# A retention and SoLU kernel: w_in cast without a stride, rows of w_out grouped anew, a new order of the instructions

## The chip, the cores and the metric

The kernel runs on one core of a Trainium2 chip. The time is in device microseconds, from the first instruction to the last, as the median of several runs. PE is TensorE (matmuls; its weight loads are shown as PEld), DVE is VectorE, ACT is ScalarE, POOL is GpSimd, and SP is the engine whose queue issues nearly all DMAs here. Each engine works through its own queue in the order in which it was given its instructions and waits for the others by semaphores.

## What is computed

```python
scores = (1 / np.sqrt(64)) * np.matmul(q, k.transpose(0, 1, 3, 2))   # 8 x 8 heads, 576 x 64
gamma = 1.0 - 2.0 ** (-5.0 - np.arange(8))
Dmat = np.where(rel >= 0, gamma[:, None, None] ** rel, 0.0)           # rel = i - j
attn = np.matmul(scores * Dmat, v)
x = attn.transpose(0, 2, 1, 3).reshape(4608, 512)

h = x @ w_in                                    # 512 -> 1024
e = np.exp(h - h.max(-1, keepdims=True))
solu = h * (e / (e.sum(-1, keepdims=True) + 1e-09))
mu, var = mean and variance of solu along the row
out = ((solu - mu) / np.sqrt(var + 1e-06) * g_ln) @ w_out           # 1024 -> 512
```

All inputs and the output are float32. The order of the 1,024 hidden columns doesn't matter to the result as long as w_in's columns, g_ln and w_out's rows follow the same one.

## The kernel before

The 576 positions of a batch are cut into two blocks of 256 and a tail of 64. A *pair* is one block of one batch (two times 128 rows of the output), or the tails of four batches together; there are 18 pairs, n = 0 to 17, and in each i = 0, 1 stands for its 128 rows. Attention is done in chunks with a carried state: for a block the scores inside a chunk, masked with the powers of gamma, and the contribution of the state.

All work is cut into named steps, and one string, `ORDER` (line 744), gives the order of all of them: `k:0.1@g` is step `k` for pair 0, half 1, on engine g (v is VectorE, s ScalarE, g GpSimd). The program runs through the string and issues each step's instructions, so each engine's queue is the string's words for that engine. `BANKS` (line 840) gives the PSUM banks in the same order. The steps that matter here:

- loads, on SP's queue: `lq`, `lk`, `lv` (line 173, 512 KB of rows of 512 bytes each, into 16 buffers `ld` used in turn), `wi` (line 647, a 512 KB slice of w_in, rows of 4 KB), `wo` (line 667, a quarter of w_out), `st` (results), `dt` and `du` (transposes by DMA)
- `q`, `k`, `v` (line 197 with a table of powers of gamma, line 152 or 150 without): casts from float32 to float16
- `tp` and `qkT`: transposes of q and k on PE and their copies out of PSUM; `sc`: scores on PE (line 265); `mk`: the masks on VectorE (line 276); `kp`, `t`, `s32`, `s16`: the state; `xs`, `xv`: x from state and from scores on PE; `xT`: its copy
- `cwA`, `cwB`: casts of the two halves of a slice of w_in
- `mm1` (line 426): h, eight matmuls of 512 columns per 128 rows, over four slices of w_in; `max` (line 434) and `solu` (line 497) on VectorE, `exp` (line 449) and `sq` (line 517) on ScalarE, `nmu`, `w1`, `w2`, `pow`: small ones for the row's mean and variance
- `lpj` and `uTj`: transposes of the result and their copies; `mm2` (line 607): the second product; `osb`: its scaling out of PSUM
- `ws`, `mean`, `mc`, `cw`: w_out times g_ln, its mean over the rows, and the difference, so that the row's mean needn't be taken off later. For the first three pairs, where `cw` isn't done yet, `uc` takes the mean off the row.
- `warm:k`: k matmuls of 512 columns on zeros; `gx`: a table by Exp on ScalarE; `small`: the tables of powers; `gln`: g_ln, with `g32` its multiple

Hidden column 8f + c is kept at place 128c + f: so w_in's cast reads with a stride of 8 numbers, and partition p of w_out holds the rows 8p + c, two of which are 4 KB without a gap. The casts, the load of w_out and the first loads read so:

```python
653:         copy(eng, w_in16[:, a, 512 * i : 512 * i + 512].rearrange("p (c f) -> p c f", c=4), src)
666:         w = moe_w_out.rearrange("(p c) m -> p c m", p=P)
850:         nc.scalar.dma_start(out=small, in_=nc.inline_tensor(small_np, name="small_c").ap())
851:         nc.scalar.dma_start(out=gln, in_=moe_g_ln.rearrange("(p c) -> p c", p=P))
```

Of the kernel before, what the change touches and what calls it, by code (L numbers as in the profile page):

```python
# [46 lines left out]
def kernel(  # L47
# [684 lines left out]
    def gx_(n, i, j, eng):  # L732
# [23 lines left out]
        xs:2.1 max:1.0 xT:2.1@s solu:1.1 mm1:2.0 lpj:0 q:3.1@g max:2.0 wo:2 wo:0 v:3.0@g g32
        k:3.1@g exp:1.0 mm1:2.1 solu:1.0 ws:4@s k:3.0@s wo:1 exp:2.0 w1:0@g v:3.1@g ws:0@g wo:3
        ws:1@g ws:5@g ws:2@s w2:0 uTj:0.1@v uTj:0.0@v ws:3@s max:2.1 lk:4 w1:1@v nmu:1.1 nmu:1.0
        ws:6@s warm:4 kp:3 ws:7@g t:3.0@s tp:3 solu:2.0 uc:1.0@v mm2:0.0 s32:3.0 qkT:3.0@s exp:2.1
        s32:2.1 qkT:3.1@s lv:4 pow:0 t:3.1 k:4.1@s sq:1.0 mean k:4.0@g sc:3.1 sc:3.0 solu:2.1  # L760
        nmu:2.0 mm2:0.1 v:4.1@v mc@s mk:3.1.0 mk:3.1.1 s16:3.0@g v:4.0@g lk:5 lk:6 mk:3.0.1
        mk:3.0.0 sq:1.1 uc:1.1@s tp:4 s32:3.1 kp:4 lq:5 qkT:4.0@s cw:5@g xv:3 qkT:4.1@s osb:0.1@v
        xs:3.1 t:4.0 warm:4 lpj:1 xT:3.1@s lq:6 cw:6@v sc:4.0 k:6.1@g nmu:2.1 xT:3.0@v s32:4.0
        k:5.1@g lv:5 uTj:1.1@s s16:1.1@s cw:0@v uTj:1.0@s osb:0.0@s t:4.1 mk:4.0.0 uc:2.0@v mm1:3.0
        w2:1 k:5.0@g q:5.1@g mm1:3.1 q:5.0@g pow:1 v:5.0@g s16:4.0@g max:3.0 uc:2.1@v s32:4.1 lk:7
        sc:4.1 q:6.0@s q:6.1@s mk:4.0.1 v:5.1@g mm2:1.0 exp:3.0 max:3.1 st:0.1 lv:6 mk:4.1.0
        mk:4.1.1 mm2:1.1 xv:4 w1:2@g xs:4.1 v:6.0@g solu:3.0 k:6.0@s v:6.1@g osb:1.0@s exp:3.1
        solu:3.1 dt:5 kp:5 t:5.0 osb:1.1@s xs:4.0 tp:6 st:1.0 s16:2.1@g cw:1@v st:0.0 sq:2.0 kp:6
        xT:4.1@s t:6.0 warm:2 lpj:2 s32:5.0 qkT:6.1@v t:5.1 xT:4.0@s qkT:6.0@s uTj:2.1@s cw:4@g
        sc:5.1 sc:5.0 uTj:2.0@s nmu:3.1 lq:8 mk:5.1.1 cw:7@v mk:5.1.0 sq:3.1 k:7.0@s sq:2.1 cw:3@v  # L770
        mk:5.0.0 mm1:4.0 max:4.0 lv:8 cw:2@g w2:2 pow:2 s32:6.0 mm1:4.1 s16:5.0@g exp:4.0 s16:6.0@g
        lq:7 mm2:2.1 lv:7 max:4.1 mk:5.0.1 solu:4.0 t:6.1 mm2:2.0 exp:4.1 k:7.1@s xs:5.1 xs:5.0
        osb:2.1@s solu:4.1 q:7.1@g sc:6.0 q:7.0@g osb:2.0@s mk:6.0.1 xv:5 v:7.1@v lk:8 lq:9 sc:6.1
        lpj:3 xT:5.0@s mm1:5.0 mk:6.1.0 uTj:3.0@s mk:6.0.0 mk:6.1.1 xs:6.0 lpj:4 nmu:3.0 w1:3@v
        max:5.0 uTj:3.1@s sq:3.0 xT:5.1@s xv:6 dt:7 xT:6.0 w2:3 xs:6.1 s32:5.1 q:8.0@g q:8.1@g
        mm2:3.1 v:8.0@g st:1.1 v:7.0@g nmu:4.1 mm2:3.0 w1:4@g k:8.1@g pow:3 q:9.0@g exp:5.0 xT:6.1
        uTj:4.1@v kp:7 uTj:4.0@s k:8.0@s lk:10 solu:5.0 osb:3.0@s nmu:5.0 sc:7.0 s16:5.1@g tp:8
        t:7.0 osb:3.1@s mm1:5.1 mk:7.0.0 sq:5.0 qkT:8.0@v nmu:4.0 sq:4.1 qkT:8.1@s sq:4.0 sc:7.1
        mk:7.0.1 lv:9 s32:7.0 mm1:6.0 max:5.1 exp:5.1 s16:7.0@g mk:7.1.1 mk:7.1.0 max:6.0 lk:9
        st:2.0 exp:6.0 st:2.1 s16:4.1@g q:9.1@g s16:3.1@g mm2:4.0 xs:7.0 s32:6.1 t:7.1 w2:4 pow:4  # L780
        mm2:4.1 st:3.0 lq:11 k:9.0@s osb:4.0@s solu:5.1 solu:6.0 xv:7 nmu:5.1 sc:8.1 osb:4.1@s
        nmu:6.0 mk:8.1.0 sq:5.1 sc:8.0 lq:10 xs:7.1 xT:7.0@s w1:5@g v:9.0@g lv:10 mm1:6.1 v:9.1@g
        k:10.1@g mk:8.0.1 s16:6.1@g s32:7.1 w2:5 mk:8.0.0 lpj:5 mm1:7.0 xT:7.1@s q:10.1@g max:6.1
        uTj:5.1@s exp:6.1 uTj:5.0@v sq:6.0 k:9.1@g k:10.0@g max:7.0 exp:7.0 mm2:5.1 mm2:5.0
        s16:7.1@g pow:5 v:8.1@g osb:5.1@s solu:6.1 lpj:6 kp:9 st:3.1 lk:11 dt:9 osb:5.0@s nmu:6.1
        mk:8.1.1 xv:8 solu:7.0 xs:8.1 t:9.0@v uTj:6.1@v sq:6.1 xT:8.1@s xs:8.0 st:4.1 lv:11 nmu:7.0
        v:10.0@g k:11.1@g q:10.0@g s32:9.0 tp:10 t:9.1 sc:9.1 mm1:7.1 xT:8.0@s v:10.1@g q:11.1@g
        qkT:10.0@s qkT:10.1@v uTj:6.0@s mk:9.1.0 mk:9.1.1 w1:6@g sc:9.0 kp:10 mm1:8.0 max:7.1
        mk:9.0.0 w2:6 t:10.0@s mk:9.0.1 lq:13 lk:12 s16:9.0@s q:11.0@g k:11.0@g s32:10.0 v:11.1@g
        max:8.0 s32:9.1 xs:9.1 v:11.0@g exp:7.1 t:10.1 mm2:6.1 pow:6 st:5.0 s16:10.0@g w1:7@g  # L790
        solu:7.1 sq:7.0 exp:8.0 mm2:6.0 k:12.1@s st:4.0 sc:10.1 solu:8.0 osb:6.1@v xv:9 mk:10.1.1
        mk:10.1.0 osb:6.0@s k:12.0@g xT:9.1@s nmu:7.1 lq:15 xT:9.0@s lpj:7 mm1:8.1 uTj:7.0@s kp:11
        uTj:7.1@v dt:11 sq:7.1 t:11.0@s st:5.1 lq:12 max:8.1 sc:10.0 mm1:9.0 w2:7 mk:10.0.1 exp:8.1
        mk:10.0.0 solu:8.1 pow:7 mm2:7.1 max:9.0 xv:10 xs:10.1 mm2:7.0 xT:10.0 s32:10.1 q:12.1@g
        xT:10.1 s32:11.0 q:13.0@g q:12.0@g q:13.1@g sc:11.1 w1:8@v osb:7.1@s lpj:8 exp:9.0 solu:9.0
        t:11.1 tp:12 lv:13 s16:11.0@s osb:7.0@s mk:11.1.1 uTj:8.0@s nmu:8.1 mm1:9.1 nmu:8.0 sc:11.0
        mk:11.1.0 uTj:8.1@s lv:12 qkT:12.0@v qkT:12.1@v v:12.0@g v:12.1@g kp:12 sq:8.1 max:9.1
        t:12.0@s st:6.1 st:7.1 mk:11.0.1 mk:11.0.0 v:13.1@g mm1:10.0 sq:8.0 max:10.0 s32:11.1
        exp:9.1 mm2:8.0 lk:14 st:6.0 mm2:8.1 s32:12.0 w2:8 t:12.1 xs:11.1 pow:8 solu:9.1 s16:9.1@s
        exp:10.0 sc:12.0 w1:9@g lk:13 lq:14 lk:15 lq:16 osb:8.0@s osb:8.1@s nmu:9.0 solu:10.0  # L800
        mk:12.0.0 xv:11 k:13.0@g xT:11.0@v sc:12.1 mk:12.1.0 xT:11.1@s mk:12.0.1 q:14.1@g k:14.1@g
        mk:12.1.1 lpj:9 k:13.1@g s16:11.1@s mm1:10.1 k:15.0@g v:13.0@g uTj:9.0@s uTj:9.1@s mm1:11.0
# [110 lines left out]
```

## Time and profile before

| | |
|---|---|
| median of 3 runs | 213.36 us (212.89 to 214.8) |
| profiled execution | 214.05 us, its span 212.3 us |
| PE busy | 196.4 us (93%) |
| DVE busy | 186.1 us (88%) |
| ACT busy | 171.0 us (81%) |
| POOL busy | 143.6 us (68%) |
| DMA | 49.29 MB in 90,530 packets, 232 GB/s in the mean |
| granted PE clock, mean | 0.983 |

The profile is of one execution. Busy time is the time in which an engine had an instruction in work; a busy PE is not a PE at its peak. The chain of waits is followed back from the last instruction: at each step to what released it, or to the instruction ahead of it on its engine. A group is a set of like instructions with the busy time, the mean of one in ns and the idle time just before them with its releaser. In a stretch, (x45) counts the instructions that began in it, and the three last columns are the clock that PE was granted, the busy share of the DMA engines and GB/s.

### The profile page before, as it was taken

Reading aid. Unit: us, or ns where it says so; the run is one execution under the profiler, and the core shown is the slowest. Engines: PE = TensorE matmul, PEld = TensorE weight load, DVE = VectorE, ACT = ScalarE, POOL = GpSimd, SP = SyncE. Lnnn points to the kernel's source line nnn. Section 1 sums busy time; section 2 is a strip of 40 time slices with the busy share of each in tenths; the row PEclk is TensorE's granted clock in tenths of the full one; section 3 lists DMA queues with packets and bytes.
Section 4 is the critical chain, followed back from the end, with each engine's and each line's share of the span. In section 5 each row is a group of like instructions: output and inputs, shape, how many; then the busy total and the mean of one; then the engine's idle time right before and its main releaser. Section 6 shows DMA issues by size and latency. Waiting matters only on the chain.

```text
span 212.3 us, 7613 instructions
## 1 busy us (share of the span) xinstructions
PE 196.4 (93%) x3154; PEld 103.2 (49%) x3154; DVE 186.1 (88%) x335; ACT 171.0 (81%) x288; POOL 143.6 (68%) x223
## 2 busy tenths in 40 slices
...
GB/s 162 290 383 310 281 296 367 295 259 262 138 217 183 213 209 216 320 293 223 249 327 164 285 236 316 279 197 246 264 203 217 238 99 179 171 148 115 85 198 150
DMA packets 90530, 49.29 MB, mean 232 GB/s; under 512 B 29440, under 2 KB 84992, under 8 KB 90496
## 3 DMA queue, kind: packets, MB, share of 16 engines
...
q10 hardware_dynamic: 368, 0.11, 0.4%
...
## 4 chain that ended last, share of the span: by engine, by line
PE 70%; DVE 14%; DMA 4%; SPq 4%; issue 3%; ACT 2%; POOL 1%; ACTq 0%; DVEq 0%; POOLq 0%
PE psum L426 25%; PE psum L607 24%; PE psum L265 5%; DVE nm L434 4%; PE psum L364 4%; DMA ld<-in_moe_w_in_dram 4%; PE psum L349 3%; PE psum L584 3%; SPq L173 3%; DVE u L497 2%; PE psum L290 2%; PE psum L239 1%; SPq L647 1%; PE psum L726 1%; DVE uc L553 1%
## 5 line engine op out<-in xcount | busy, mean ns | idle before, releaser
L426 PE MATMUL psum<-w_in,xT 128*128 128x512 f16 x280 | 68.5, 390 | 1.6 <-issue 0.7
L607 PE MATMUL psum<-w_out,uTj 128*128 128x512 f16 (+1 forms) x248 | 55.1, 372 | 0.0
L434 DVE TENSOR_REDUCE nm<-psum 128x1 f32<-128x1024 f32 x35 | 42.5, 1218 | 6.5 <-PE psum L426 6.1
L449 ACT ACTIVATE e<-psum,nm 128x1024 f32<-128x1024 f32 x35 | 39.0, 1114 | 11.0 <-DVE nm L434 9.2
L607 PEld LDWEIGHTS <-uTj 128*128 128x128 f16 x296 | 28.0, 98 | 31.0 <-issue 0.6
L497 DVE SCALAR_TENSOR_TENSOR u<-psum,e 128x1024 f16<-128x1024 f32 x35 | 42.0, 1216 | 0.4 <-ACT e L449 0.3
L517 ACT ACTIVATE sq<-u,nmu 128x1024 f16<-128x1024 f16 x35 | 40.3, 1150 | 1.2 <-DVE nmu L507 0.9
L426 PEld LDWEIGHTS <-xT 128*128 128x128 f16 x280 | 25.8, 100 | 31.3 <-issue 4.7
L540 POOL TENSOR_TENSOR rs<-w,mhalf 128x2 f32<-128x2 f32 x17 | 11.8, 696 | 38.0 <-DVE w L528 36.7
L197 POOL TENSOR_TENSOR v<-ld,small 128x512 f16<-128x512 f32 x29 | 30.4, 1057 | 4.6 <-DMA ld<-in_v_dram 3.5
L197 POOL TENSOR_TENSOR qk<-ld,small 128x512 f16<-128x512 f32 x24 | 25.0, 1050 | 1.1 <-DMA ld<-in_q_dram 0.6
L150 ACT COPY uTj<-psum 128x1024 f16<-128x1024 f16 (+1 forms) x18 | 17.3, 990 | 3.1 <-PE psum L584 3.1
L314 POOL TENSOR_TENSOR s32a<-t,small 128x256 f32<-128x256 f32 x16 | 10.6, 662 | 11.8 <-DVE t L152 6.9
L726 PE MATMUL psum<-s16s 128*128 128x512 f16 x50 | 14.2, 429 | 3.5 <-DVE s16s L853 3.1
L152 POOL CAST qk<-ld 128x512 f16<-128x512 f32 x25 | 15.4, 628 | 0.7 <-DMA ld<-in_k_dram 0.6
L150 ACT COPY qkT<-psum 128x1024 f16<-128x1024 f16 x12 | 12.0, 1018 | 4.7 <-PE psum L239 4.7
L265 PE MATMUL psum<-qkT 64*64 64x128 f16 x576 | 14.7, 223 | 0.2
L150 ACT CAST xT<-psum 128x512 f16<-128x512 f32 x24 | 13.3, 588 | 1.7 <-PE psum L349 1.0
L265 PEld LDWEIGHTS <-qkT 64*64 64x64 f16 x576 | 9.8, 107 | 7.5 <-issue 6.3
L364 PEld LDWEIGHTS <-v 64*64 64x64 f16 x576 | 9.3, 106 | 7.1 <-issue 6.8
L349 PE MATMUL psum<-qkT,s16s 128*128 128x128 f16 (+1 forms) x128 | 10.7, 216 | 1.6 <-POOL s16s L152 1.4
L314 POOL TENSOR_TENSOR s32b<-t,small 128x256 f32<-128x256 f32 x16 | 10.2, 640 | 2.0 <-DVE t L305 1.8
...
## 6 DMA issues: line engine op xcount, KB each, us to landing
...
```

The lines of the kernel that those rows point to most:

```text
L150: nc.scalar.copy(out=out, in_=in_)
L197: vec(eng).tensor_tensor(out=to, in0=src, in1=tab[:, 8 * e : 8 * e + 8].unsqueeze(2).to_broadcast([P, H, D]), op=ALU.mult,)
L265: nc.tensor.matmul(out=s[o][cc, hp], lhsT=qkT_view(n, 1, c)[dd, e, hp], rhs=qkT_view(n, 0, c)[dd, :, hp], start=True, stop=True,)
L314: nc.gpsimd.tensor_tensor(out=s, in0=T["t", n, i], in1=gs.unsqueeze(2).to_broadcast([P, 4, D]), op=ALU.mult)
L349: nc.tensor.matmul(out=to, lhsT=state[:, hp].rearrange("p e d -> p (e d)"), rhs=rhs, start=first and hp == 0 and j == 0, stop=True, skip_g ...
L364: nc.tensor.matmul(out=x[c][oo, hp], lhsT=v16[cc, e, 2 * hp + o], rhs=T["ret", n, e, o][cc, hp], start=first[c] and e == 0 and hp == 0, st ...
L426: nc.tensor.matmul(out=h[:, a], lhsT=s[:, d], rhs=w_in16[:, d, a * 512 : (a + 1) * 512], start=r == 1, stop=r == 4,)
L434: nc.vector.tensor_reduce(out=nm, in_=T[key("h", n, i, j)], axis=AX.X if j is not None else AX.XY, op=ALU.max, negate=True)
L449: nc.scalar.activation(out=flat(e, j), in_=T[key("h", n, i, j)], func=ACT.Exp, bias=T["nm", n, i], accum_out=s)
L497: nc.vector.scalar_tensor_tensor(out=flat(u, j), in0=T[key("h", n, i, j)], scalar=1.0, in1=flat(T[key("e", n, i, j)], j), op0=ALU.mult, op ...
L517: nc.scalar.activation(out=t, in_=T[key("u", n, i, j)], func=ACT.Square, bias=T["nmu", n, i], accum_out=ss)
L607: nc.tensor.matmul(out=o, lhsT=T["uT", n, i][:, c], rhs=wt[:, c, a : a + w], start=c == 0, stop=c == NF - 1,)
```

## The change

Four things, apart from the order:

- w_in is cast without a stride, hidden columns keep their places.
- Partition p of w_out holds the rows 128c + p (a row is 2 KB), and g_ln is loaded to match, one number per place.
- `small` and `gln` become steps of the order on SP's queue (before: ACT's queue, at the start); the memsets and tables on POOL (`consts`, `tris`) become steps too.
- a new `ORDER` and new `BANKS`; eight `warm` words become eleven, with 50 matmuls on zeros before and 38 after. 89 steps that stay change their engine.

```diff
     def cast_w_in(a, i, eng):
-        src = T["w_in32", a].rearrange("p (f c) -> p c f", c=NF)[:, 4 * i : 4 * i + 4]
-        copy(eng, w_in16[:, a, 512 * i : 512 * i + 512].rearrange("p (c f) -> p c f", c=4), src)
+        copy(eng or "s", w_in16[:, a, 512 * i : 512 * i + 512], T["w_in32", a][:, 512 * i : 512 * i + 512])
...
+    def small_(n, i, j, eng):
+        nc.sync.dma_start(out=small, in_=nc.inline_tensor(small_np, name="small_c").ap())
+
+    @step
+    def gln_(n, i, j, eng):
+        with nc.allow_non_contiguous_dma("1024 numbers"):
+            nc.sync.dma_start(out=gln, in_=moe_g_ln.rearrange("(c p) -> p c", p=P))
...
-        w = moe_w_out.rearrange("(p c) m -> p c m", p=P)
+        w = moe_w_out.rearrange("(c p) m -> p c m", p=P)
...
     ORDER = """
-        lk:0 gx lq:0 k:0.0@s k:0.1@g q:0.0@v lv:0 lq:1 q:0.1@v warm:21 tp:0 v:0.1@v v:0.0@v kp:0
-        q:1.1@v t:0.0@v s32:0.0 qkT:0.1@v qkT:0.0@s lk:1 k:1.0@v q:1.0@g warm:6 sc:0.0 t:0.1 wi:2
-        k:1.1@s sc:0.1 wi:0 wi:3 s32:0.1 mk:0.1.0 warm:4 tp:1 mk:0.0.0 mk:0.0.1 cwB:2@s s16:0.0@s
-        mk:0.1.1 xv:0 cwA:2@g wi:1 qkT:1.1@v cwA:0@v cwB:0@g xT:0.0@v cwB:3@g qkT:1.0@s sc:1.0
-        mk:1.0.1 xs:0.1 cwA:3@s mm1:0.0.3 lv:1 cwA:1@g xT:0.1@v s16:0.1@g cwB:1@s v:1.1@g mk:1.0.0
-        sc:1.1 mm1:0.0.0 lq:2 lk:2 q:2.1@g q:2.0@g mk:1.1.0 mm1:0.1 v:1.0@v mk:1.1.1 k:2.0@g
-        max:0.1 exp:0.1 mm1:0.0.2 mm1:0.0.1 max:0.0 k:2.1@v kp:1 t:1.0@s warm:7 tp:2 s32:1.0 lv:2
...
+        tris consts lq:0 small lk:0 lv:0 k:0.0@v q:0.1@g k:0.1@g q:0.0@v lk:1 tp:0 v:0.0@g v:0.1@v
+        lq:1 kp:0 qkT:0.1@v t:0.0@v wi:1 q:1.1@g k:1.1@g qkT:0.0@s q:1.0@v cwB:1@s cwA:1@s sc:0.1
+        warm:5 sc:0.0 k:1.0@v tp:1 mk:0.1.0 mk:0.0.0 wi:2 mk:0.0.1 mk:0.1.1 wi:3 warm:4 xv:0
+        s32:0.0 t:0.1 cwA:2@g s16:0.0@s qkT:1.0@s cwB:2@s xs:0.1 xT:0.1@s qkT:1.1@v cwB:3@g wi:0
+        lv:1 cwA:0@s xT:0.0@s lq:2 s32:0.1 cwA:3@v gx cwB:0@g sc:1.1 warm:3 sc:1.0 mm1:0.1
+        mm1:0.0.1 s16:0.1@g mm1:0.0.2 mm1:0.0.0 mk:1.1.1 mk:1.0.1 mk:1.0.0 v:1.0@g mk:1.1.0 v:1.1@g
+        mm1:0.0.3 max:0.1 max:0.0 q:2.0@g q:2.1@g lk:2 kp:1 exp:0.1 solu:0.1 k:2.0@s t:1.0@s
+        s32:1.0 k:2.1@s s16:1.0@v warm:9 tp:2 warm:2 xv:1 xs:1.1 lv:2 lq:3 qkT:2.1@v v:2.1@g t:1.1
+        exp:0.0 qkT:2.0@s v:2.0@g sc:2.1 solu:0.0 xT:1.0@s nmu:0.0 kp:2 xT:1.1@s gln t:2.0@s lk:3
+        lk:4 s32:1.1 sc:2.0 lv:3 wo:1 s16:1.1@g q:3.1@g s32:2.0 nmu:0.1 mk:2.1.0 wo:3 mk:2.0.1
+        mk:2.1.1 mm1:1.1 wo:0 uc:0.0@s sq:0.1 q:3.0@g mm1:1.0 max:1.1 mk:2.0.0 sq:0.0 exp:1.1 xv:2
+        w1:0@v xT:2.0@s s16:2.0@g g32 v:3.1@g v:3.0@g xs:2.1 max:1.0 k:3.1@s xT:2.1@s k:3.0@s
+        exp:1.0 solu:1.1 mm1:2.0 ws:2@s w1:1@g ws:3@s uc:0.1@v t:2.1 nmu:1.1 warm:1 mm1:2.1 max:2.0
+        solu:1.0 warm:2 tp:3 warm:6 kp:3 wo:2 exp:2.0 sq:1.1 ws:4@s ws:0@v solu:2.0 ws:6@g ws:7@g
+        ws:1@g qkT:3.0@v lpj:0 ws:5@g qkT:3.1@s max:2.1 lq:4 uTj:0.0@s uTj:0.1@v lv:4 s32:2.1
+        nmu:1.0 t:3.0@v mean mm2:0.1 nmu:2.0 uc:1.0@v w2:0 k:4.1@g q:4.0@g s32:3.0 exp:2.1 sc:3.1
+        mc@s k:4.0@s q:4.1@g v:4.0@g pow:0 sc:3.0 lq:5 lk:5 t:3.1 v:4.1@g s16:3.0@g solu:2.1 cw:1@v
+        mk:3.0.0 mk:3.0.1 mk:3.1.0 mk:3.1.1 cw:0@v t:4.0 xT:3.0@v cw:5@v mk:4.0.0 nmu:2.1 cw:6@v
...
-        nc.scalar.dma_start(out=small, in_=nc.inline_tensor(small_np, name="small_c").ap())
-        nc.scalar.dma_start(out=gln, in_=moe_g_ln.rearrange("(p c) -> p c", p=P))
+    def consts(n, i, j, eng):
         nc.gpsimd.iota(place, pattern=[[1, P]], base=0, channel_multiplier=0)
         nc.vector.memset(s16s, 0.0)
```

More of the change, by code (lines that the diff above doesn't have):

```diff
@@ L756 @@
[L756 to L802, printed above, removed]
@@ new lines @@
+        s32:4.0 q:6.1@s k:6.0@g cw:5@v lv:5 mk:4.0.0 nmu:2.1 cw:6@v max:3.0 mk:4.0.1 s32:3.1
+        mm1:3.1 s16:4.0@g t:4.1 uTj:1.1@s v:5.0@g mm2:1.1 s32:4.1 max:3.1 w2:1 pow:1 v:6.1@g
+        exp:3.0 k:6.1@s solu:3.0 uc:2.1@v q:6.0@s warm:2 tp:6 sc:4.1 exp:3.1 dt:5 mk:4.1.1 xs:4.1
+        mk:4.1.0 solu:3.1 osb:1.1@s v:5.1@g qkT:6.1@v uc:2.0@s cw:2@g warm:1 mm2:1.0 kp:5 lq:7
+        xs:4.0 xv:4 sq:2.1 q:7.0@g t:5.0 cw:3@v kp:6 osb:1.0@s t:6.0 s32:5.0 w1:3@g cw:4@g
+        qkT:6.0@s lpj:2 sc:5.1 cw:7@v w2:2 nmu:3.0 xT:4.1@s mk:5.1.1 mk:5.1.0 xT:4.0@s mm1:4.0
@@ new lines @@
+        q:7.1@g lv:7 t:5.1 uTj:2.0@s st:0.0 lk:8 pow:2 s16:2.1@g sc:5.0 max:4.0 uTj:2.1@s st:0.1
+        lk:7 mm1:4.1 k:7.0@g mm2:2.1 s32:6.0 mk:5.0.0 mk:5.0.1 max:4.1 s16:5.0@s sq:3.0 s32:5.1
+        v:7.0@g exp:4.0 mm2:2.0 solu:4.0 xs:5.0 k:7.1@s xs:5.1 xv:5 exp:4.1 osb:2.0@s osb:2.1@v
+        v:7.1@g solu:4.1 t:6.1 sc:6.1 sc:6.0 nmu:3.1 xT:5.0@s s16:6.0@g s16:3.1@g mk:6.1.1 lpj:3
+        xT:5.1@s xs:6.0 mk:6.0.0 uTj:3.1@v mk:6.1.0 mm1:5.0 mk:6.0.1 sq:3.1 uTj:3.0@s lpj:4 lq:8
+        lk:10 lk:9 st:1.1 kp:7 xv:6 dt:7 uTj:4.1@s max:5.0 xT:6.0 xs:6.1 q:8.1@g xT:6.1 w2:3
@@ new lines @@
+        nmu:4.1 mm2:3.1 exp:5.0 k:8.0@s s16:4.1@s s32:6.1 uTj:4.0@v k:8.1@g mm2:3.0 pow:3 st:1.0
+        solu:5.0 q:8.0@g w1:4@v lq:10 osb:3.1@s nmu:4.0 sc:7.0 t:7.0 osb:3.0@v s32:7.0 mk:7.0.0
+        sq:4.0 tp:8 mm1:5.1 qkT:8.0@v sq:4.1 nmu:5.0 sc:7.1 mk:7.0.1 w2:4 mm1:6.0 max:5.1 mk:7.1.1
+        q:10.0@s qkT:8.1@s s16:6.1@g k:10.0@g mm2:4.1 xs:7.0 st:2.0 mk:7.1.0 k:9.1@g lq:9 lq:11
+        st:2.1 exp:5.1 pow:4 max:6.0 sq:5.0 exp:6.0 k:9.0@g solu:5.1 t:7.1 s16:7.0@g q:11.1@g
+        mm2:4.0 osb:4.1@s solu:6.0 sc:8.1 q:10.1@g lv:9 nmu:6.0 osb:4.0@s mk:8.1.1 nmu:5.1 q:9.0@v
@@ new lines @@
+        xv:7 mk:8.1.0 sc:8.0 s32:7.1 lv:8 q:9.1@g lpj:5 mk:8.0.0 xT:7.0@s s16:5.1@g v:8.0@g sq:6.0
+        mm1:6.1 uTj:5.0@s max:6.1 q:11.0@g mk:8.0.1 uTj:5.1@s sq:5.1 xs:7.1 mm1:7.0 exp:6.1
+        s16:7.1@s w1:5@g k:10.1@g w2:5 mm2:5.1 max:7.0 exp:7.0 v:9.0@g xT:7.1@s lk:11 st:3.0 st:3.1
+        solu:6.1 st:4.0 v:9.1@g pow:5 dt:9 nmu:6.1 mm2:5.0 osb:5.0@s lpj:6 uTj:6.0@s k:11.1@s lv:10
+        osb:5.1@v kp:9 k:11.0@g v:8.1@g xv:8 solu:7.0 sc:9.1 uTj:6.1@v w1:6@v mk:9.1.0 t:9.0@v
+        mk:9.1.1 xs:8.0 xT:8.0@s mm1:7.1 s32:9.0 xs:8.1 sq:6.1 v:10.1@g tp:10 sc:9.0 xT:8.1@s lv:11
@@ new lines @@
+        v:10.0@v nmu:7.0 t:9.1 max:7.1 mm1:8.0 s16:9.0@g w2:6 mk:9.0.1 qkT:10.1@s kp:10 qkT:10.0@s
+        exp:7.1 t:10.0@s lk:12 mk:9.0.0 max:8.0 mm2:6.0 mm2:6.1 w1:7@v solu:7.1 s32:9.1 pow:6
+        s32:10.0 st:4.1 lq:12 st:5.0 t:10.1 nmu:7.1 exp:8.0 xv:9 sc:10.1 sq:7.0 solu:8.0 lpj:7
+        osb:6.1@v osb:6.0@s mk:10.1.1 xs:9.1 q:12.0@g v:11.1@g xT:9.0@s k:12.1@s xT:9.1@s k:12.0@s
+        mm1:8.1 v:11.0@g uTj:7.0@v kp:11 uTj:7.1@v sq:7.1 mk:10.1.0 lq:13 t:11.0@s st:5.1 lq:15
+        max:8.1 sc:10.0 s16:10.0@g dt:11 mm1:9.0 w2:7 mk:10.0.1 exp:8.1 mk:10.0.0 solu:8.1 pow:7
```

142 lines of the change are left out of this document (77 added, 65 removed).

## The prediction

> **What bounds the kernel now.** I read the page's chain of waits first, then the chain in order of time, then busy time in stretches whose borders I set at the places where the chain changes engine. The chain in order of time, up to the first softmax row (start, length, what):
>
> ```profile
> 5.12 1.76 SPq L173
> 6.93 1.74 SPq L647
> 8.71 0.43 SPq L647
> 9.19 8.22 DMA ld<-in_moe_w_in_dram
> 17.43 1.13 ACT w_in L150
> 18.61 1.01 PE psum L426 x2
> 19.62 0.57 PE psum L265 x12
> 20.19 4.37 PE psum L426 x10
> 24.58 1.24 DVE nm L434
> 25.84 1.21 ACT e L449 x2
> ```
>
> To be seen: until 24.58 us the end is set by loads, the cast of w_in, and ten matmuls at 0.43 us each; then VectorE takes over. The stretches (length, busy time per engine, granted clock, DMA share):
>
> ```profile
> 14.30:17.80 3.50, 2.06 (x74) 1.53 (x66) 3.50 (x7) 2.69 (x5) 2.94 (x4) 0.97 1.04 372
> 17.80:21.20 3.40, 2.86 (x24) 1.04 (x22) 3.18 (x6) 1.88 (x2) 3.06 (x5) 0.50 1.16 289
> 21.20:24.80 3.60, 3.60 (x10) 1.27 (x9) 1.99 (x3) 0.00 (x0) 3.02 (x4) 0.56 1.13 286
> 24.80:28.20 3.40, 3.17 (x74) 1.55 (x72) 3.40 (x4) 2.36 (x4) 0.96 (x3) 1.00 1.06 276
> 51.30:90.90 39.60, 37.26 (x684) 20.41 (x684) 37.70 (x65) 34.72 (x55) 36.97 (x50) 1.00 0.90 215
> 90.90:207.10 116.20, 115.46 (x1764) 61.14 (x1762) 105.82 (x203) 101.02 (x180) 68.33 (x112) 1.00 0.92 215
> ```
>
> Three regimes, then. Up to 24.58: loads, and a PE clock that was cut to 0.50 at 17.8 and opened at 24.8. From 24.58 to 90.9 (the last mask of pair 7): VectorE, 26.18 of 26.70 us busy up to 51.3 (the last mask of pair 3) and 37.70 of 39.60 behind it. From 90.9: PE, 115.46 of 116.20. What comes late at 90.9 comes late at the end. Groups by form give the casts:
>
> ```profile
> L150 ACT CAST qk<-ld 128x512 f16<-128x512 f32 x17 | 10.3, 612 | 1.0 <-DMA ld<-in_k_dram 1.0
> L152 POOL CAST w_in<-ld 128x512 f16<-128x512 f32 x4 | 4.4, 1115 | 0.8 <-DMA ld<-in_moe_w_in_dram 0.8
> L150 ACT CAST w_in<-ld 128x512 f16<-128x512 f32 x3 | 3.4, 1122 | 1.6 <-DMA ld<-in_moe_w_in_dram 1.6
> ```
>
> **The loads.** SP's issues (start plus time to landing) land at 5.2, 7.1, 8.9, 10.7, 12.5; the slices of w_in at 13.7, 15.0, 17.4, 18.75; lv:1 at 20.5, lq:2 22.3, lk:2 24.3, lv:2 26.1, the next at 27.8. The title speaks of two slices ahead of the second pair's loads and two behind. The order as written doesn't have that: before and after, q and k of pair 1 go ahead of all four slices and lv:1 behind them. So w_in is whole at 18.75 in both, and lq:2, lk:2, lv:2 keep their places: 0 us. `small` moves from ACT's queue to SP's, behind lq:0. Queue 10 held 368 packets in 0.4% of 16 engines' 212.3 us, 37 ns each, so its 128 packets are 128 x 37 / 16 = 0.3 us of transfer, which ran on the same engines before; I take 0, bounds 0 and 0.3.
>
> `gln` becomes 1,024 numbers that are 128 apart on a partition's row, so 1,024 packets of 4 bytes behind lq:3. At 37 ns: 64 x 37 = 2.4 us per engine; at a 512-byte row's pace (1,024 packets in 1.75 us) 1.75; no row shows 4 bytes, so double (4.7) is the upper bound. All loads behind it shift by that; none ahead does. Rows of w_out fall from 4 KB to 2 KB, 512 packets more: nothing, or up to 512 x 27 / 16 = 0.9 us. Who waits: wo:0, third of the four, lands at 27.8 + 2.4 + 3 x 1.75 (lk:3, lk:4, lv:3) + 3 x 1.57 (the mean of the w_in slices) = 40.2; VectorE wants it (ws:0, behind solu:1.0) at 41.6 in the count below. The cover is 1.4 us; at double the price 0.9 us shows. The Trainium skill, DMA: Bandwidth & Descriptors, rules for kernel authors, speaks against this edit: a last dimension that isn't contiguous becomes one descriptor per element. It gives no price per element, and the trace of before has no such transfer.
>
> **The casts of w_in.** Without the stride the same form on the same engine costs 0.61 on ACT (612) and 0.61 to 0.63 on POOL, against 1.12. Seven of eight save 0.5 us each, but only the last lies on the path: 18.75 + 0.61 = 19.4 against 18.77 + 1.12 = 19.9. Gain 0.5 us.
>
> **The start of PE.** The 21 matmuls on zeros ran 3.11 to 9.88, and tp:0 stood behind them until 9.81 though its casts were done at 8.5. After: k:0.0 (0.42) at 7.1 and q:0.0 (0.69) on VectorE, tp:0 at 8.2. That 1.6 us doesn't arrive: VectorE has q:1.0 and k:1.0 ahead of the first mask, and lq:1 lands at 12.5; 12.5 + 0.69 + 0.42 = 13.6 against 14.03. Four masks to 16.05, xv and xs to 17.6, xT:0.1 to 18.2; sc:1.1 to 18.1, three warming matmuls (0.43) to 19.4, sc:1.0 (0.6) to 20.0.
>
> Now the clock. In before, PE was 2.06 of 3.50 us busy in 14.3 to 17.8 and lost the clock; 2.86 of 3.40 in the next stretch didn't give it back; 3.60 of 3.60 did. Before 20.0 the new order has 12 warming matmuls for 31, so full stretches are few: I take a cut clock until 24.8, as in before. mm1:0.1 (8 x 0.427 = 3.42) then ends at 23.4, mm1:0.0 at 25.9 (three slow, five at 0.22). The first max starts 1.2 us early, the second 0.2 late.
>
> **VectorE from the first max to pair 3's last mask.** Counting its queue, with the mean durations of the groups: before 8 mk (0.62), 6 max (1.18), 6 solu (1.19), 5 nmu (0.15), 3 t (0.41), 3 v and q (0.69), k (0.42), 2 uc (0.66), 2 uTj (0.64), w1, w2 (0.6): 26.9 us, where the trace took 26.7. After: the same mk, max, solu, nmu, uc; 4 t, 2 qkT (0.68), one uTj, s16 (not shown on VectorE: 0.4 to 0.8 by ACT's copies of 0.40, I take 0.5), ws (0.5, between VectorE's cast of that size, 0.42, and ACT's ws, 0.71), cw (0.7), w1, w2: 27.2. Its waits: max:0.0 on mm1, 24.6 to 25.9 or 26.0 (1.4); solu:2.0 on exp:2.0, since ACT has k:3.1, xT:2.1, k:3.0, exp:1.0, ws:2 and ws:3 (0.61, 0.59, 0.61, 1.31, 0.7, 0.7) in front and ends exp:2.0 at 42.9, VectorE being free at 42.1 (0.8). 23.4 + 27.2 + 2.2 = 52.8, against 51.3: 1.5 us late.
>
> From there to pair 7's last mask both queues hold the same: 38.2 us before, 38.5 after. Behind it VectorE gets 3.3 us more (112.5 against 109.2: xT:15.1, xT:17.1, uTj:8.0, uTj:9.0 and small ones come to it), beside PE, in a stage where it idles 116.2 - 105.8 = 10.4 us. That idle time hides it; if it doesn't, see the third rival. PE's own work there is unchanged, the warming matmuls all lie ahead of it.
>
> **Sum.** -0.5 (cast) and -0.7 (less waiting ahead of mm1) make the -1.2 at the first max; +0.3 of work, +2.2 of waits and +0.2 (my 26.9 against the trace's 26.7) make +1.5 at 51.3, carried to the end. The profiled execution took 214.05 (span 212.3), 0.69 above the median of 213.36; on the median: 214.9.
>
> **Rivals.** (1) The clock is open before mm1:0.1. For it: from 10.6 on PE is almost never idle in the new order. Against it: the stretch with 2.86 of 3.40. mm1:0.1 runs 19.4 to 21.2. VectorE starts 3.4 us early, but lk:2 still lands at 24.3 and ACT has k:2.0, t:1.0, k:2.1 ahead of exp:0.0 (25.9 to 27.2, where before had it end at 28.4); its waits come to 0.7 + 0.4 + 0.2 + 0.4 + 1.0 = 2.7, so 21.2 + 27.2 + 2.7 = 51.1: -0.2, 213.2. The Trainium skill, TensorE: Matmul & The Clock Gate, on the warm-up, has the clock open after some 3.4 us of sustained matmuls, however few they are. By that the clock would open near 14 to 17 here and this rival would hold; the stretch 17.8 to 21.2 speaks against a generous reading of "sustained".
>
> (2) Faster: as (1), and VectorE stays packed as it is today (0.5 idle in 26.7). 21.2 + 27.2 + 0.5 = 48.9: -2.4, 211.0; down to 210 if the cover holds better behind 51.3 too. It decides when VectorE's waits there stay under 1 us.
>
> (3) Slower: VectorE, not PE, sets the pace behind 90.9. It has 3.3 us more to do, and its 10.4 us of idle time are waits for PE and ACT, spread over 203 instructions; if they stay what they are, the whole 3.3 is added: 214.9 + 3.3 = 218.2. It decides when VectorE's idle time there stays near 10 instead of falling to 7. Against it: PE 115.46 of 116.20.
>
> **Numbers.** Forecast 0.42 (its own range 213.2 to 216.8: the price of gln, s16 and the waits by a microsecond or two); rival 1 0.20; rival 2 0.15; rival 3 0.23. A measurement here tells 1% from no change: 211.2 to 215.5. Faster: rival 2, 0.14. Within 1%: rival 1 and some 0.24 of the forecast's 0.42, 0.45 with a little from rival 2. Slower: the rest, 0.41. The range leaves out half of rival 2 and the end of rival 3: 211.0 to 218.6.
>
> **What would show it.** The last w_in slice lands at 18.7 to 18.8; its cast on ACT or POOL takes 0.61; clock 0.50 at 20 to 23; first max at 23.4, exp:0.0 near 27.6, pair 3's last mask at 52.8; packets 90,530 + 896 + 512 = 91,938, gln landing 2 to 3 us behind lq:3. A clock of 1.00 at 20 us makes it rival 1 or 2; a DMA wait on w_out ahead of ws makes gln dearer than taken; VectorE idle over 10 us behind pair 7 makes it rival 3.

## The result and the profile after

| | before | after |
|---|---|---|
| median | 213.04 us (20 runs, 210.93 to 215.79) | 215.62 us (20 runs, 213.71 to 217.74) |
| ratio | | 1.0131, 95% interval 1.01 to 1.0161 |
| profiled execution | 214.05, span 212.3, mean clock 0.983 | 213.89, span 212.2, mean clock 0.994 |
| PE, DVE busy | 196.4, 186.1 us | 190.5, 187.0 us |

The changed kernel is slower by 1.3%, while the two profiled executions take the same time. That is the first thing to read: the profile of before is an execution 1.0 us above its median, that of after one 1.7 us below its own. What differs between them, and between executions of one kernel, has to be found before the two profiles can be subtracted. Medians are of all runs; the ratios, and the tables by mean clock further down, leave out executions more than 1.5% above the fastest of their kernel.

The same stretches of after as were shown of before (length, busy time per engine with the instructions that began, granted clock, DMA share, GB/s):

```profile
14.30:17.80 3.50, 3.22 (x88) 2.19 (x88) 3.43 (x7) 2.90 (x6) 1.67 (x4) 1.00 1.05 370
17.80:21.20 3.40, 2.88 (x41) 1.35 (x30) 2.80 (x5) 2.72 (x7) 2.92 (x6) 1.00 1.16 291
21.20:24.80 3.60, 3.60 (x48) 1.63 (x47) 2.70 (x3) 2.17 (x5) 3.60 (x4) 1.00 1.11 277
...
51.30:90.90 39.60, 35.48 (x628) 19.27 (x621) 36.49 (x64) 33.49 (x54) 36.00 (x48) 1.00 0.98 241
90.90:207.10 116.20, 115.31 (x1763) 61.65 (x1762) 108.36 (x206) 101.29 (x180) 64.66 (x101) 1.00 0.91 210
```

The clock is open at 17.8 to 24.8, where before had 0.50 and 0.56. From 51.3 to 90.9 both PE and VectorE stand still more than before: PE 4.12 us for 2.34, VectorE 3.11 for 1.90. Behind 90.9 VectorE has 2.5 us more to do and PE is as full as it was.

The chain in order of time (start, length, what; a few of its rows up to 50 us):

```profile
14.44 9.76 DMA ld<-in_k_dram
24.22 0.62 ACT qk L150
...
34.93 0.52 ACT qk L150
...
37.87 2.65 POOL w_raw L694 x3
...
41.05 1.04 POOL w_raw L694
```

Where before went from mm1 straight to VectorE at 24.58, after's chain runs through the load of lk:2, its cast, and POOL's products with w_out. Casts and packets:

```profile
L150 ACT CAST w_in<-ld 128x512 f16<-128x512 f32 x4 | 2.4, 617 | 3.8 <-DMA ld<-in_moe_w_in_dram 3.8
L152 POOL CAST w_in<-ld 128x512 f16<-128x512 f32 x3 | 2.1, 695 | 1.8 <-DMA ld<-in_moe_w_in_dram 1.8
```

```profile
DMA packets 91938, 49.29 MB, mean 232 GB/s; under 512 B 30336, under 2 KB 85888, under 8 KB 91904
```

The steps that the prediction named, in five profiles whose clock was not cut between its opening and the last stores (before's was, so it stands apart). Of the others, e3 and e9 have the old order, e7 and e11 are the changed kernel again; all are described below:

| start of, us | before | e3, e9 (old order, new layout) | after, e7, e11 (changed kernel) |
|---|---|---|---|
| first max | 24.58 | 21.81, 22.67 | 21.53, 21.51, 21.27 |
| exp:0.0 | 27.20 | 24.41, 25.26 | 25.53, 25.61, 25.34 |
| end of pair 3's last mask | 51.32 | 49.34, 49.47 | 49.93, 50.23, 49.78 |
| mk:7.1.0 | 90.33 | 88.63, 88.39 | 89.58, 90.48, 90.17 |
| span | 212.3 | 211.3, 209.6 | 212.2, 213.0, 213.2 |

### The profile page after: what moved, and what is told of

It is laid out like the page before. It is cut to its first block, busy times and chain, and to the rows that moved or that the text cites. A ratio compares the mean times of both kernels' runs of the same rounds, so it can differ in the third digit from the quotient of the medians.

```text
span 212.2 us, 7577 instructions
## 1 busy us (share of the span) xinstructions
PE 190.5 (90%) x3142; PEld 102.2 (48%) x3142; DVE 187.0 (88%) x338; ACT 171.2 (81%) x293; POOL 141.6 (67%) x214
## 2 busy tenths in 40 slices
DMA packets 91938, 49.29 MB, mean 232 GB/s; under 512 B 30336, under 2 KB 85888, under 8 KB 91904
## 4 chain that ended last, share of the span: by engine, by line
PE 63%; POOL 9%; DVE 6%; SPq 6%; ACT 5%; DMA 5%; issue 3%; ACTq 0%; POOLq 0%; DVEq 0%
PE psum L607 25%; PE psum L426 21%; DMA ld<-in_k_dram 5%; SPq L173 4%; PE psum L364 4%; PE psum L265 3%; PE psum L349 3%; PE psum L584 3%; PE psum L290 2%; POOL w_raw L694 2%; POOL v L197 2%; POOL qk L197 2%; SPq L647 1%; ACT sq L517 1%; DVE u L497 1%
## 5 line engine op out<-in xcount | busy, mean ns | idle before, releaser
L426 PE MATMUL psum<-w_in,xT 128*128 128x512 f16 x280 | 65.6, 380 | 1.6 <-ACT xT L150 0.6
L197 POOL TENSOR_TENSOR v<-ld,small 128x512 f16<-128x512 f32 x33 | 35.9, 1099 | 5.8 <-DMA ld<-in_v_dram 5.5
L540 POOL TENSOR_TENSOR rs<-w,mhalf 128x2 f32<-128x2 f32 x17 | 12.3, 722 | 35.9 <-DVE w L528 35.7
L197 POOL TENSOR_TENSOR qk<-ld,small 128x512 f16<-128x512 f32 x25 | 27.4, 1101 | 2.8 <-DMA ld<-in_q_dram 2.0
L150 ACT COPY uTj<-psum 128x1024 f16<-128x1024 f16 (+1 forms) x17 | 16.1, 968 | 0.9 <-PE psum L584 0.8
L152 POOL CAST qk<-ld 128x512 f16<-128x512 f32 x22 | 14.2, 651 | 2.4 <-DMA ld<-in_k_dram 2.2
L314 POOL TENSOR_TENSOR s32a<-t,small 128x256 f32<-128x256 f32 x16 | 10.4, 652 | 7.4 <-ACT t L150 3.1
L239 PE MATMUL psum<-ident,qk 64*128 64x64 f16 x320 | 7.1, 199 | 8.4 <-DVE qk L197 8.4
L150 ACT CAST qk<-ld 128x512 f16<-128x512 f32 x20 | 12.4, 629 | 0.3 <-DMA ld<-in_k_dram 0.2
```

Of the source, the lines that this page charges most:

```text
L150: nc.scalar.copy(out=out, in_=in_)
L152: vec(eng).tensor_copy(out=out, in_=in_)
L197: vec(eng).tensor_tensor(out=to, in0=src, in1=tab[:, 8 * e : 8 * e + 8].unsqueeze(2).to_broadcast([P, H, D]), op=ALU.mult,)
L314: nc.gpsimd.tensor_tensor(out=s, in0=T["t", n, i], in1=gs.unsqueeze(2).to_broadcast([P, 4, D]), op=ALU.mult)
L426: nc.tensor.matmul(out=h[:, a], lhsT=s[:, d], rhs=w_in16[:, d, a * 512 : (a + 1) * 512], start=r == 1, stop=r == 4,)
```

## The experiments

The theory at the start was that of the forecast: without the 21 matmuls on zeros PE's clock opens late, or closes again, in part of the executions, and the front is late then. The rivals were the order itself (VectorE's stretch, the late stage) and the layout of w_out and g_ln.

**More and fewer warming matmuls in the new order: e1, e8, e5.**

```diff
e1:  lk:1 tp:0   ->   lk:1 warm:21 tp:0
e8:  lk:1 tp:0   ->   lk:1 warm:10 tp:0
e5:  warm:5, warm:4 and warm:3 ahead of mm1 removed
```

> The changed kernel with 21 warming matmuls put back ahead of its first transposes. Theory order (VectorE's waits between the first max and the last mask of pair 7 carry the loss): 215.6 us as the changed kernel, within 0.5. Theory clock (the missing warming matmuls leave PE's clock cut when mm1 of pair 0 runs, in most executions): 213.2 to 214.0, with a granted clock of 1.00 at 17 to 24 us in the profile.

> The changed kernel with 10 warming matmuls ahead of tp:0 instead of 21: 4.3 us of work at the cut clock from 3.1 us on, up to 7.4, less than a microsecond ahead of tp:0. Theory clock: if 4 us of work are enough to open it, as the kernel of before shows (21 matmuls, open at 7.3), 213.5, as with 21; if it then closes again in the pause until tp:0, 214.5 to 215.6.

> The changed kernel without its three warming steps ahead of mm1 (12 matmuls), which leaves PE less busy between 10 and 20 us. Theory clock: the clock opens only while mm1 runs, at 22 to 26 us, the first max starts at 23 or later (21.5 in the profile of the changed kernel) and the time is 216.5 to 217.5. Theory order (the time is set behind 25 us and the early clock doesn't matter): 215.6, as the changed kernel.

e1: 213.46 us, ratio 1.0021 (0.9984 to 1.0058): most of the loss is gone. e8: 215.97, 1.0104 (1.0067 to 1.0142): nothing gained. e5: 216.92 (4 runs), 1.0142 (1.0087 to 1.0196), as the clock theory expected, with the first max at 23.27. The rows of e5, where the clock opened at 23.2 (the last three columns begin with the granted clock):

```profile
19.80:23.20 3.40, 3.40 (x9) 1.22 (x8) 1.16 (x2) 1.84 (x5) 2.92 (x5) 1.00 1.10 275
23.20:26.60 3.40, 3.40 (x47) 1.53 (x45) 2.71 (x3) 2.07 (x5) 1.78 (x3) 1.00 1.04 237
```

The clock column says 1.00 in both, although the trace's first clock record is the opening at 23.2; the counts show it: 9 matmuls fill the first 3.40 us, mm1's at 0.43 us each as in before, and 47 begin in the next. So the numbers of e1 and e5 agree with the clock theory. e8's lies above both of its values: in its profile the clock opened at 8.0, was cut again from 11.5 to 14.9 and was open from there, and the first max came at 21.62, as in the changed kernel (21.53). What e8 loses is not at the front. The profiles of these runs show where, further down.

**The layout, in both orders: e2, e3.** e2 is the changed kernel with the strided casts and the old grouping of w_out and g_ln; e3 is the old order with the new ones, and `gln` on SP behind lq:3.

```diff
e2:
-    copy(eng or "s", w_in16[...], T["w_in32", a][:, 512 * i : 512 * i + 512])
+    src = T["w_in32", a].rearrange("p (f c) -> p c f", c=NF)[:, 4 * i : 4 * i + 4]
+    copy(eng, w_in16[...].rearrange("p (c f) -> p c f", c=4), src)
-    w = moe_w_out.rearrange("(c p) m -> p c m", p=P)
+    w = moe_w_out.rearrange("(p c) m -> p c m", p=P)
e3: the reverse of these lines in the kernel before, and  lq:3 lk:3  ->  lq:3 gln lk:3
```

> The changed kernel's order with the layout of before: strided casts of w_in, partition p of w_out and of g_ln with the rows 8p + c, so that g_ln is 128 packets. Theory order: 0.5 us slower than the changed kernel (216.1), the strided cast of the last slice. Theory transfers (1,024 packets of 4 bytes and the shorter rows of w_out hold up loads): 1 us or more faster, 214.5 or less.

> The order of before with the new layout: casts of w_in without a stride, w_out rows 128c + p, g_ln as 1,024 numbers on SP's queue behind lq:3. Theory order: 0.5 us faster than before, 212.5, from the last cast alone. Theory transfers: slower than before by 1 us or more, 214 or above, with ws waiting for a load of w_out.

e2: 217.44, 1.0222 (1.0153 to 1.029), so without the layout the new order is 0.9% slower still, slower than either theory expected; its first max comes 0.68 us later than after's and max:1.1 1.07. e3: 212.93, 0.9983 (0.9943 to 1.0023). The layout costs nothing that can be measured in the old order and helps in the new one. The loss lies in the order.

**The clock in the old order: e4, e6.**

```diff
e4:  tp:1 -> tp:1 warm:3      xs:0.1 -> xs:0.1 warm:2      mm1:0.0.3 -> mm1:0.0.3 warm:2
e6:  warm:21 tp:0 -> tp:0
```

> The kernel of before with seven more warming matmuls (3 behind tp:1, 2 behind xs:0.1, 2 behind the first two matmuls of mm1) where PE stood idle between 14 and 19.5 us. Theory clock: the granted clock stays at 1.00 from 17 to 25 us and the time falls by about 2 us, to 211, since ten matmuls at 0.43 us end the chain at 24.6. If the cut clock is no part of the path: 213.0, unchanged within 0.5.

> The mirror image: the kernel of before without its 21 warming matmuls at the start, all else as it was. Theory clock: about 2 us slower than before, 215 to 216, as the changed kernel is. If the changed kernel loses for another reason: 213.4 within 0.5, or faster, since tp:0 no longer stands behind the warming matmuls for 1.3 us.

e4: 213.21, 1.0003 (0.9961 to 1.0045); e6: 213.03, 0.9978 (0.9948 to 1.0008). Both expectations of the clock theory missed. In e4's profile, of an execution 2.5 us above its median, the front was right (open at 17 to 25, first max at 22.62 for 24.58) and the gain was gone at 109, behind a stop of PE's; in e6 the 21 matmuls turned out not to be needed. As it stood, the theory had fallen: something other than the front takes the time.

**Further profiles of the changed kernel: e7, e10, e11.** Nothing is edited in them.

> The changed kernel once more, for its time beside the others on one chip and a second profile. Theory clock: 215.6, 1.2% above before, and a granted clock that opens at another time than 15.0 us, with the first max moving with it, by up to 2 us.

> The changed kernel as it is, one more profile. The theory that executions differ by the stretches in which the clock is cut expects: an execution with the clock open from 15 or 16 on and no cut has the first max at 21.5 and a span of 212 to 213; each stretch of 3.4 us with a cut clock on a busy PE adds about 1.7 us; one that opens late, at 20 or later, has the first max at 22.5 to 23.5 and the end 1.5 to 2 later. The rival, that the 1% is in the order and not in the clock, expects the same first max and mean clock whatever the time.

> As the one before: a further profile of the changed kernel as it is. Span 212 to 213 with no cut stretch before 207, 213.5 to 215 with one.

e7: 215.15 us, 1.0074 (1.0034 to 1.0114), so the loss is 0.7% here, for 1.3% in the first comparison, and e1's 0.2% has to be set against both. e10 and e11, one time each: 216.34 and 214.90. e7's clock opened at 15.97, 1.0 later than in the first profile, but its first max came at 21.51 as there: the expected move stayed out. e10 has one cut, at 82.4, and a span of 214.6; e11 has none and 213.2. Together with the first runs they allow a comparison at equal mean clock (medians of the single times):

| mean granted clock | before | after | difference |
|---|---|---|---|
| 0.994 and more | 212.22 (15 runs) | 214.71 (15) | 2.5 |
| 0.989 to 0.994 | 213.30 (14) | 215.90 (9) | 2.6 |
| 0.983 to 0.989 | 213.74 (26) | 215.97 (7) | 2.2 |
| below | 214.08 (5) | none | |

So the changed kernel loses some 2.5 us at equal mean clock, and its mean clock is higher than that of the kernel before, not lower. This speaks against cuts as the cause. It says nothing of late openings: the mean counts no time ahead of the first clock record, which came at 7.3 in before's profile and at 14.0 to 16.0 in the four of the changed kernel. Against those stand e6 and the first maxima of these four, all at 21.1 to 21.5; the other executions have no profile. A fuller clock alone doesn't shorten the time either: nine of the ten runs of e4 that count here lie at 0.994 and more, and their median is 213.08, for 212.22 of the kernel before. And e1, all of whose runs but one lie at 0.994 and more, has 213.39 there: 1.3 us better than after at the same clock.

**Where PE stands.** After's chain between 76 and 82 us:

```profile
76.41 1.73 PE psum L426 x8
78.14 0.57 PE psum L584 x32
78.71 0.37 PE psum L290 x32
79.08 0.06 PE psum L364 x4
79.14 1.54 issue
80.68 0.59 PE psum L364 x28
```

In the midst of xv:6, after 4 of its 32 matmuls, PE stands for 1.54 us and waits for nothing that the profile shows: "issue". It isn't a mask that is late: pair 6's last one had ended at 78.41, and the next matmuls read the two masks that the first four had read. What the DMA queues did from 78.3 to 79.4 has a packet of another kind in it:

```profile
q1 hardware_dynamic: 191, 0.25, 79.0%
q8 instruction: 1, 0.02, 5.5%
```

One of the 24 packets of 16 KB of queue 8 (0.39 MB in the page's list) runs from 78.34 to 79.31. PE has 3,142 matmuls and as many weight loads, 262 of these per packet. If this queue brings PE's instructions, a stop should lie at a fixed count of instructions whatever the program does there. It does (PE's and PEld's columns are the matmuls and the weight loads begun since the start), in after, in e8 and in before:

```profile
0.00:79.20 79.20, 64.65 (x1246) 35.44 (x1247) 68.89 (x113) 60.21 (x98) 68.17 (x100) 1.00 1.00 268
...
79.80:83.20 3.40, 2.52 (x41) 1.48 (x41) 1.90 (x5) 2.28 (x5) 1.55 (x3) 1.00 1.01 307
```

```profile
0.00:65.00 65.00, 54.94 (x991) 28.36 (x991) 54.66 (x91) 48.68 (x80) 54.18 (x81) 0.97 1.00 274
0.00:79.90 79.90, 68.19 (x1246) 35.89 (x1247) 69.27 (x113) 60.26 (x98) 68.63 (x101) 0.98 1.02 263
```

```profile
0.00:66.50 66.50, 57.26 (x991) 28.97 (x992) 57.76 (x94) 48.19 (x76) 52.75 (x82) 0.95 0.97 269
0.00:81.00 81.00, 70.85 (x1247) 36.86 (x1248) 71.37 (x117) 60.28 (x94) 66.48 (x97) 0.96 0.97 254
0.00:110.00 110.00, 99.29 (x1759) 52.08 (x1759) 97.92 (x166) 86.16 (x139) 91.87 (x139) 0.97 0.99 260
```

The rows are cut inside stops. Two orders with different steps stop at 991, 1,246 or 1,247 and 1,759 matmuls: 255 and 513 apart. e8's ten matmuls more and e5's twelve fewer don't move the stop in the count (e5: 991), they move it to another step of the program. The time from one matmul to the next at these stops, and from the end of the packet to the next matmul:

| | at matmul | start to start, us | packet's end to next matmul |
|---|---|---|---|
| after, e7, e10, e11 | 1,246 | 1.76, 2.30, 2.57, 1.51 | 1.37, 1.53, 1.44, 1.29 |
| e2 (same PE instructions) | 1,246 | 2.58 | 1.38 |
| before | 991, 1,247, 1,759 | 1.09, 0.95, 1.12 | 1.44, 1.48, 1.62 |
| e8 | 991 and 1,246 | 1.76 and 2.56 | 1.55 and 1.29 |
| e5 | 991 | 2.73 | 1.42 |
| e3, e4 (old order) | 1,759 | 1.77, 2.56 | 1.38, 1.58 |
| e1 (21 matmuls more) | 1,246 | 0.54 | 1.49 |

In e1 the count 1,246 is reached 0.8 us later in the run, in a kp; the packet ended at 78.77, 0.95 before PE came to that count, and the stop is nearly gone. Where a packet ended still earlier there is none: 2.2 us ahead of that count in e9, 2.7 in e6, 4.5 in e12. e1's chain at the same place:

```profile
79.10 0.57 PE psum L584 x32
79.67 0.24 PE psum L290 x15
79.92 0.35 issue
80.26 0.32 PE psum L290 x17
```

Whether this is what e1 gains is not shown: in its profile pair 3's last mask ends at 50.88, 0.95 later than after's, the stretch from there to mk:7.1.0 takes 38.47 us, 1.18 less, and the two profiled executions are equally long (212.1 and 212.2).

**And what a stop does to the clock.** e10 is after's twin up to 78 us (max:5.0 at 78.05 for 78.33) and ends 2.4 us later:

```profile
79.00:82.40 3.40, 1.20 (x35) 0.87 (x35) 0.84 (x2) 2.79 (x6) 1.52 (x3) 1.00 0.95 278
...
82.40:85.80 3.40, 3.40 (x10) 1.19 (x9) 3.04 (x10) 0.59 (x2) 1.91 (x3) 0.50 1.09 305
```

PE was busy for 1.20 us of 3.40, and the next 3.40 were granted half the clock. Between max:5.0 and max:5.1 e10 takes 2.49 us more than after: 0.81 by the longer stop (2.57 for 1.76) and 1.7 by 3.4 us at half speed. The rest of the run is 2.2 later. In before, the same happens at the front:

```profile
14.20:17.60 3.40, 1.96 (x80) 1.43 (x71) 3.40 (x7) 2.60 (x5) 2.84 (x4) 0.99 1.04 380
17.60:21.00 3.40, 2.86 (x25) 1.13 (x24) 3.18 (x7) 2.08 (x2) 3.06 (x5) 0.50 1.16 290
21.00:24.40 3.40, 3.40 (x10) 1.19 (x9) 1.98 (x2) 0.00 (x0) 2.82 (x4) 0.50 1.13 282
```

The cuts in the clock records last 3.41 us each ahead of the kernel's end, 6.83 in before, and what lies between opening and cut is a multiple of that (68.27 us, or 20 times, in e10). Laying windows of 3.4 us over every profile, with borders where its own clock changed, gives nearly one rule for all of them. Windows followed by a cut had PE busy for 0.66 us (e12), 1.17 and 1.58 (e8), 1.20 (e2, e4, e10), 1.21 (e5), 1.68 (e6) and 1.96 (before). The emptiest windows that weren't followed by one had 2.00 (e9), 2.01 (e3), 2.10 (e7), 2.12 (e11) and 2.52 (after). One window doesn't fit: at the very end of e9 1.45 us of large matmuls were followed by no cut until a window later; busy time is not quite what is counted. With that reserve, the stops of 2.56 to 2.73, each with most of its length in one window, were followed by a cut (e2, e4, e5, e8, e10), those of 1.5 to 2.3 weren't. Whether a long one that a border halves would be is not shown. This ties the two halves together: in these profiles the mean clock of an execution follows from where PE stood. The Trainium skill, TensorE: Matmul & The Clock Gate, Part 1, has such a free-running window of some 3.4 us and lets the clock fall behind an idle one. Here PE needn't be idle for a window, less than 2.0 us of work in it was enough.

**The best of the parts: e9**, e3 without the 21 matmuls.

```diff
- q:0.1@v warm:21 tp:0 v:0.1@v
+ q:0.1@v tp:0 v:0.1@v
```

> The old order with the new layout of w_in, g_ln and w_out, and without the 21 matmuls on zeros ahead of the first transpose. If the two edits add (0.9983 for the layout, 0.9978 without the 21), the ratio is 0.996 and the time about 212.7 to 212.9. If the layout's gain at the front hangs on the clock that the 21 matmuls open, the ratio is 1.000 to 1.003. The first max is expected at 21.5 to 23.0.

212.95 us, 0.9972 (0.9939 to 1.0006): between the two expectations, and not to be told from the kernel before. Its profile is of a quick execution, 211.27, with neither cut nor long stop, and shows what the old order can do:

```profile
51.30:90.90 39.60, 37.73 (x657) 20.43 (x657) 38.34 (x66) 34.84 (x56) 36.51 (x50) 1.00 0.98 235
90.90:204.00 113.10, 113.10 (x1749) 59.91 (x1747) 104.40 (x199) 98.75 (x175) 67.50 (x110) 1.00 0.94 216
```

PE idles 1.87 us in the middle and not at all behind it.

**POOL's products ahead of w1:1: e12**, e1 with two moves that should have shortened VectorE's stretch up to pair 3.

```diff
POOL:  ws:2@s w1:1@g ws:3@s ... ws:1@g ... ws:5@g   ->   ws:2@s ws:3@s ... ws:1@g ... ws:5@g w1:1@g
SP:    lk:3 lk:4 ... wo:2   ->   lk:3 ... wo:2 lk:4
```

> The new order with the 21 matmuls on zeros, and two more moves: w1:1 on POOL goes behind the steps ws:6, ws:7, ws:1 and ws:5, and the load lk:4 on SP goes behind the last quarter of w_out (wo:2), which so lands about 1.7 earlier. If the new order's VectorE stretch up to pair 3's last mask is stretched by POOL's products of w_out that come late (28.4 to 29.6 where the old order has 26.7), it shrinks by 1 to 1.5 and the time goes from 213.46 to about 212.3. If it is the clock alone, the time stays at 213.5. If SP's loads for pair 4 become the new wait, lk:4's casts come late and the time is 214 or more.

217.28 us, 1.0142 (1.0088 to 1.0196): slower. The stretch took 28.62 us for e1's 29.56, close to the shrinking by 1 to 1.5 that was expected; but after, without these moves, has 28.40 and e7 28.72, so it is e1's profile that stands apart, and what the moves did to the stretch is not shown. The loss comes 20 us later. ACT's and SP's waits there (engine, line, what it waited for, us, times, longest):

```profile
ACT qk L150 <- DMA ld<-in_k_dram: 4.2, 1, 4.2
```

```profile
SPq L173 <- DVE w_out L721: 5.4, 1, 5.4
```

The loads use 16 buffers in turn. lk:4 behind wo:2 changes which tile each later load inherits; a load in SP's queue then waits 5.4 us for a cw on VectorE to give its buffer free, those behind it wait too, and lk:7 keeps ACT waiting for 4.2. The third expectation named the engine and the direction, not the place. The two moves were not run one by one; it is these waits that put the loss on lk:4.

## Why the prediction was right and where it wasn't

The forecast of 214.9 was 0.7 low and its range holds. Slower is what came, which had 0.41; the largest chance, 0.45, stood on a time within 1%. Its mechanism came about in part only, so step by step:

**Loads, packets, casts: right.** 91,938 packets, the last casts of w_in begin at 18.9 and 19.0, and a cast takes 0.62 on ACT and 0.61 on POOL at the median.

**The price of gln: wrong, and outside its bounds.** gln was issued at 22.31 and landed at 28.3; lq:3 ahead of it landed at 28.1 (so gln came 0.2 behind it, not 2 to 3) and lk:3 behind it at 30.1, 2.0 later where a load took 1.75. In the trace a packet of 4 bytes takes 9 ns, so 1,024 x 9 / 16 = 0.58 us of each DMA engine, and the load behind came some 0.25 us late, not 2.4 (bounds 1.75 to 4.7). The packets whose time I took, 37 ns for some 300 bytes and 27 for a 512-byte row, were no near rows: a packet of 4 bytes took a third of that or less. The rule of the Trainium skill, DMA: Bandwidth & Descriptors, rules for kernel authors (one descriptor per element), is seen in the packet count, 91,938 as summed up. The transfer was not worth a term here. w_out was in time for VectorE: its only waits between 21.5 and 49.9 are these 1.3 us.

```profile
DVE nm L434 <- PE psum L426: 1.3, 3, 0.6
```

**The clock at the front: the forecast's case exists, but isn't what the profile shows.** With the clock closed until 23.2 (e5) the first max is at 23.27, for 23.4 in the sum. In after, e7, e10 and e11 it opened between 14.0 and 16.0 and the first max came at 21.1 to 21.5: the first rival's 21.2. The rival's reason holds: in after PE was never idle from 10.6 to the opening at 14.99, and 2.88 of 3.40 us at 17.8 to 21.2 didn't close the clock again.

**VectorE's stretch: right in after's work, too dear in waits.** 27.2 of work and 2.2 of waits were taken; VectorE was busy for 27.36 of the 28.40 us in after, so it waited for 1.04. That the work came out so near is luck: the pair of s16 took 1.44 instead of 0.5, and the count of before's queue by the same means, 26.9, was too high, since the profile has 26.2 busy of 26.7. So the terms of +0.3 and +0.2 stood for some 1.1 us more work. Of the waits, that for mm1 was 0.57 instead of 1.4, and that of solu:2.0 on exp:2.0 didn't occur. Pair 3's last mask ended at 49.93, between the first rival's 51.1 and the second's 48.9, and not at 52.8. Against the old order with an open clock (49.34, 49.47) that is 0.5 late, against the shown profile 1.4 early.

**"From there to pair 7's last mask both queues hold the same": this is the step that failed.** The stretch was taken to be VectorE's, with 38.5 us for 38.2. It took 39.65 in after, 40.25 in e7, 39.0 in before, 38.9 and 39.3 in e9 and e3. VectorE idles 3.1 us there, 1.8 of them in one wait for xv right behind PE's stop. PE idles 4.12 us in after, 4.79 in e7, 4.45 in e11, for 2.34 in before, 2.18 in e3 and 1.87 in e9. Two rows make up the difference: the stop at matmul 1,246 (1.3 to 2.1 us idle; 0.7 in before and 0.6 in e3 at the same count), and sc:4.1, which waits 1.3 us for solu:3.0 to leave its PSUM bank, in after, e1, e7, e8 and e11; in before, e3 and e9 PE waits 0.2 us at most for a solu there. Of after:

```profile
DVE xT L386 <- PE psum L364: 1.8, 1, 1.8
PE psum L364 <- issue: 1.5, 1, 1.5
PE psum L265 <- DVE u L497: 1.3, 1, 1.3
```

And of before:

```profile
PE psum L364 <- issue: 0.7, 1, 0.7
PE psum L349 <- DVE u L497: 0.2, 1, 0.2
```

e1 has the wait of sc:4.1 but only 0.35 us of the stop, and its stretch took 38.47, no longer than in the old order: in this profile the wait for the bank alone made nothing late. Equal queues on the engine that bounds a stage don't make equal times when another engine feeds it.

**The late stage: right on VectorE.** It got 2.5 us more (108.36 for 105.82), forecast 3.3, and idled 7.8 instead of 10.4; PE was at 115.31 of 116.20. The third rival, 218.2, didn't come. From mk:7.1.0 to the end the profiles take 122.5 to 123.0 us in the new order, 122.7 in e3 and 121.2 in e9.

**The sum: the base was off.** The forecast set the profile of before 0.69 above its median as a constant. It was an execution with a cut at the front. Against it after's profile is at -0.2, which is what the first rival gave. The median is 2.6 worse since at a mean clock of 0.994 and more the old order takes 212.2 and the new one 214.7. That the forecast's +1.5 stands near +2.6 is partly luck: its late front is worth -1.4 on the profiles and +0.5 between open clocks, and the rest arises behind 51, where it had nothing. By the table of steps, the three profiles of the changed kernel are on average 0.6 us behind e3 and e9 at pair 3's last mask, 1.6 at mk:7.1.0 and 2.3 at the end. The failed step is worth some 1.0 of this; for the last 0.8 no cause was found, and e3 has as long a late stage as after.

**What stays open.** That queue 8 brings PE's instructions is inferred, from the fixed counts and from the 1.29 to 1.62 us between a packet's end and PE's next matmul in the table. No kernel was run that shifts PE's stream without touching when its clock opens, so it is not shown how much of e1's 1.3 us at equal mean clock is the stop. Nor was sc:4.1's bank taken away.
